# Keys of the first head group loaded in two transfers, its first queries cast and transposed in two pieces

## The chip, the cores and the metric

The kernel runs on one core of a Trainium2 chip. The metric is the device time of one execution in microseconds. The core's engines work side by side and meet at semaphores: PE (matmuls, with weight loads ahead of them), DVE and ACT (elementwise work, casts, transposes on DVE), POOL (elementwise work, and the issue of transfers that change the type on the way) and SP (which here only issues transfers). Each engine takes its instructions in the order in which the program holds them.

## The reference

Sigmoid attention over 8 batches of 12 heads with 448 positions and 64 columns, then a two-layer network on the 3584 tokens that come out:

```python
def _attn_ref(q, k, v):
    scores = scale * np.matmul(q, k.transpose(0, 1, 3, 2)) - np.log(S)
    attn = 1.0 / (1.0 + np.exp(-scores))
    return np.matmul(attn, v)

x = attn_out.transpose(0, 2, 1, 3).reshape(B * S, H * D)      # 3584 x 768

def _moe_ref(x, w_in, w_out, beta):
    h = x @ w_in                                              # 768 x 2048
    g = h * (1.0 / (1.0 + np.exp(-beta * h)))
    return g @ w_out                                          # 2048 x 768
```

All inputs and the output are float32; the kernel computes on float16 tiles with float32 sums.

## The kernel before

Heads are taken in groups of four, three groups to a batch, so that 128 partitions hold 4 heads times 32 rows. For a group, queries and keys lie in a `raw` tile of 128 partitions by 2 by 14 chunks of 64 columns: row r = 0 is the queries, r = 1 the keys, and `NB` = 14, `NH` = 7, `D` = 64. Before the scores can be formed, both are transposed by DVE in blocks of 32 (`transpose`, lines 200 and 212): the queries into `qT`, in halves of 7 chunks in the first group, the keys into `kT` by two instructions, the first over chunks 0 to 8, the second over chunks 8 to 14. `rows_of(0)` gives (0, 4), from which these 8 chunks come. A score matmul (L229) takes its weights from `kT` and streams `qT`; ACT turns score tiles in PSUM into float16 weights of the attention (`weigh`, L242, later `weigh_two`, L257); a further matmul with the values (L335) gives a tile of x, which DVE casts out of PSUM (L349). The two layers of the network (L379, L410, L524, L652) are woven between the score matmuls as filling work for PE, by a hand-written list of unit counts. Results leave through SP (L711).

The order of the start is written out by hand, inside a manual schedule, as the list `BEGIN`. Each entry is a few instructions on one or two engines, and entries stand in each engine's queue in this order:

- `("cast", r, c0, c1, act)` casts chunks c0 to c1 of group 0's keys or first half of queries from a float32 staging area (in the tile `gt`, which is not yet needed) into `raws[0]`, on ACT (L833) or DVE (L835).
- `("k", 0)` and `("q", 0, 0)` are the transposes of group 0's keys and of its first query half.
- `("idle", 20)` are 20 matmuls of 256 columns on zeros (L849), which need no input; they stand ahead of the first scores in PE's queue. `("busy", n)` are n such matmuls of 448 columns between scores (L854).
- `("scores", 0, h, s)` are score matmuls for query half h of group 0, with the ACT instructions behind them.
- `("beta",)` transposes the beta vector on DVE (L868).

Group 0's keys and first query half come in as float32 through SP's queue (L824); they are followed there by the beta vector (L856). All other loads (the second query half, the groups behind, the values, the weights) are issued by POOL (L125, L154, L169), with the keys of group 1 first.

Of the kernel before, what the change touches and what calls it, by code (L numbers as in the profile page):

```python
# [13 lines left out]
def kernel(  # L14
# [14 lines left out]
    B, H, S, D = q.shape  # L29
# [4 lines left out]
    HQ = P // BLK  # L34
    NB = S // BLK
# [106 lines left out]
    def rows_of(i: int):  # L142

        n = JF + int(i < KL // BLK)
        return i * JF + min(i, KL // BLK), n
# [14 lines left out]
    def double_v_last(b: int):  # L160
        assert all((b, "full", t, i) in ready for t in range(QPB) for i in range(KL // BLK))
        ready.add((b, "v"))
        nc.vector.tensor_copy(out=vs[b][KL:P, :, JF], in_=vs[b][0:KL, :, JF])
# [25 lines left out]
    def in_order(b: int, t):  # L189
        t = t.rearrange("p c e -> p (c e)").bitcast(FP32)  # L190
        return t.rearrange("p (q c) -> p c q", c=NB) if b == B - 1 else t

    def transpose(g: int, r: int, c0: int = 0, c1: int = NB):
        raw = raws[g][:, r]
        assert g or (r, c0) == (0, NB // 2) or all((r, "cast", c) in ready for c in range(c0, c1))
        if r == 0:
            if g not in qT:
                qT[g] = qTp.tile([P, NB * BLK, PAIR], FP16, tag="qT", name="qT")
            ready.update((g, "q", c) for c in range(c0, c1, NB // 2))
            nc.vector.transpose(  # L200
                out=in_order(g // QPB, qT[g][:, c0 * BLK : c1 * BLK]),
                in_=raw[:, c0:c1].rearrange("p c d -> p (c d)").bitcast(FP32),
            )
            return
        ready.add((g, "k"))
        kT[g] = kTp.tile([P, S, PAIR], FP16, tag="kT", name="kT")
        to = kT[g].rearrange("p k e -> p (k e)").bitcast(FP32)
        frm = raw.rearrange("p c d -> p (c d)").bitcast(FP32).rearrange("p (c f) -> p c f", c=NB)
        half = to.rearrange("p (x i q) -> p x i q", i=2, q=BLK)
        for i in (0, 2):  # L210
            c, n = rows_of(i)
            nc.vector.transpose(  # L212
                out=half[:, i // 2 :: 2].rearrange("p j i q -> p i j q"),
                in_=frm[:, c : c + 2 * n].rearrange("p (i j) f -> p i j f", j=n),
            )
# [78 lines left out]
    def half_visit(g: int, c0: int, second: int):  # L294
        slots = (2 * g, 2 * g + 1)
        scos = [score_tile() for _ in slots]
        plan = [(s, jt, sco, jt * QH) for jt in (0, 1) for s, sco in zip(slots, scos)]
        widths = [S, S]
        if second:
            plan = [(s, 2, sco, 0) for s, sco in zip(slots, scos)]  # L300
            plan += [(s, JF, scos[1], QH) for s in slots]
            widths = [QH, S]
        for i in range(0, len(plan), 2):
            for e in range(PAIR):
                for s, jt, sco, u0 in plan[i : i + 2]:
                    for hh in range(2):
                        score(sco, u0, s, jt, hh, e, c0, QH)
        if len(scored) == 2 and not second:
            two = weigh_two(ps[:, 0:4, 0:S], ())
            ats = dict(zip(map(id, scos), two if n_sc[0] % 2 == 0 else two[::-1]))  # L310
        else:
            ats = {id(sco): weigh(sco, n) for sco, n in zip(scos, widths)}
        for s, jt, sco, u0 in plan:
            at_use(ats[id(sco)], (s, jt, c0), slice(u0, u0 + QH))
# [3 lines left out]
    def attend(g: int, c0: int, n: int, keys=None):  # L318

        b, t = divmod(g, QPB)  # L320
        if b not in xTs:
            xTs[b] = xTp.tile([P, NHC, S], FP16, tag="xT", name="xT")
        assert (b, "v") in ready and (b, "full", t, HQ - 1) in ready
        slots = (2 * g, 2 * g + 1)
        if (g, c0) not in opened:
            opened[g, c0] = [bank(n, (g, s)) for s in slots], []
        avs, done = opened[g, c0]
        if keys is None:
            keys = [JF, *range(JF)] if n == S else [*range(JF), JF]
        for jt, i in [(jt, i) for jt in keys for i in range(2)]:  # L330
            s, av = slots[i], avs[i]
            at = at_take((s, jt, c0))
            base, nk = (last_base(s), KL) if jt == JF else (0, P)
            for hh in range(2):
                nc.tensor.matmul(  # L335
                    av[hh * D : (hh + 1) * D, 0:n],
                    vs[b][base : base + nk, 2 * (s % NPAIR) + hh, jt],
                    at[base : base + nk, hh, 0:n],
                    start=not done and jt == keys[0],
                    stop=len(done) + len(keys) > JF and jt == keys[-1],  # L340
                    tile_position=(base, hh * D),
                )
        done.extend(keys)
        if len(done) <= JF:
            return
        del opened[g, c0]
        for s, av in zip(slots, avs):
            touch(held.pop((g, s)))
            nc.vector.tensor_copy(out=xTs[b][:, s % NPAIR, c0 : c0 + n], in_=av)  # L349
        for s in slots:  # L350
            ready.update((b, s % NPAIR, c) for c in range(c0, c0 + n, QH))
# [433 lines left out]
    def fill_units(n: int):  # L785
        for _ in range(n):
            fill[at_fill[0]][1]()
            at_fill[0] += 1

    NH = NB // 2  # L790
    share_psum(3)
    with tc.manual_schedule():
# [27 lines left out]
        staged = gt[:, 0:4].rearrange("p c w -> p (c w)").bitcast(FP32)  # L820
        raws[0] = rawp.tile([P, 2, NB, D], FP16, tag="raw", name="raw")
        parts = {1: (staged, NB), 0: (staged[:, NB * D :], NH)}
        for r, (to, n) in parts.items():
            nc.sync.dma_start(  # L824
                out=to[:, 0 : n * D],
                in_=(q, k)[r][0, 0:HQ].rearrange("h (p c) d -> (h p) (c d)", c=NB)[:, 0 : n * D],
            )

        def cast(r: int, c0: int, c1: int, act: bool):
            out = raws[0][:, r, c0:c1].rearrange("p c d -> p (c d)")  # L830
            frm = parts[r][0][:, c0 * D : c1 * D]
            if act:
                nc.scalar.copy(out=out, in_=frm)  # L833
            else:
                nc.vector.tensor_copy(out=out, in_=frm)  # L835
            ready.update((r, "cast", c) for c in range(c0, c1))
# [10 lines left out]
        def idle_units(n: int):  # L847
            for _ in range(n):
                nc.tensor.matmul(idle[:, 0:256], still[:, 0:P], still[:, 0:256], start=True, stop=True)  # L849

        def busy_units(n: int):
            to = bank()
            for _ in range(n):
                nc.tensor.matmul(to, still[:, 0:P], still[:, 0:S], start=True, stop=True)  # L854
# [5 lines left out]
        def loads():  # L860
            for x in LATER:
                load(*x)

        def beta_columns():
            ready.add("beta")
            for i in range(P // BLK):
                part = slice(i * BLK, (i + 1) * BLK)
                nc.vector.transpose(out=beta_sb[part], in_=beta_in[:, part])  # L868

        BEGIN = [  # L870
            ("cast", 1, 0, 8, False), ("cast", 1, 8, 14, True), ("cast", 0, 0, 7, True), ("k", 0), ("q", 0, 0),
            ("idle", 20), ("scores", 0, 0, 1), ("busy", 2), ("scores", 0, 0, 0), ("busy", 2), ("busy", 4),
            ("q", 0, 1), ("q", 1, 1), ("scores", 0, 1, 0), ("busy", 4), ("busy", 4), ("q", 1, 0),
            ("scores", 0, 1, 1), ("busy", 2), ("beta",), ("k", 1), ("visit", 1, 0), ("busy", 1), ("v", 0),
# [7 lines left out]
        for what, *a in BEGIN:  # L882
            if what == "q":
                g, half = a
                transpose(g, 0, half * NH, (half + 1) * NH)
            elif what == "k":
                transpose(a[0], 1)
            elif what == "scores":
                half_visit(a[0], a[1] * QH, a[2])
            elif what == "cast":  # L890
                cast(*a)
            elif what == "idle":
                idle_units(a[0])
            elif what == "busy":
                busy_units(a[0])
            elif what == "v":
                double_v_last(a[0])
            elif what == "half":
                attend(a[0], a[1] * QH, QH)
            elif what == "values":  # L900
                attend(a[0], 0, S, a[1:])
            elif what == "visit":
                visit(*a)
            elif what == "dense":
                fill_units(a[0])
            elif what == "beta":
                beta_columns()
            elif what == "loads":
                loads()
            elif what == "two":  # L910
                share_psum(2)
# [152 lines left out]
```

## Time and profile before

| | |
|---|---|
| median of 3 runs | 369.52 us (369.27 to 369.52) |
| profiled execution, own time | 369.46 us |
| its span, first to last instruction | 367.7 us |
| PE busy | 362.2 us (99%) |
| DVE busy | 262.7 us (71%) |
| ACT busy | 258.5 us (70%) |
| POOL busy | 83.4 us (23%) |
| granted TensorE clock, mean | 0.999 |

The page gives busy time for each engine over the whole span, so a short stage has to be read from the trace itself: by windows (busy time of each engine in a stretch), by the chain of work that ended last, and by single instructions in order of time. In such rows the first number is the start and the second the length, in microseconds from the start of the span; a bracket tells how long the engine stood idle ahead of the instruction, and what ended that. SPq rows are issues of transfers, whose data lands later. Group rows give the busy time in microseconds and the mean of one instruction in nanoseconds.

### The profile page before, as it was taken

To read this page: it belongs to the slowest core of one execution; us is meant where nothing else is said; L and a number is where in the kernel's file an instruction comes from. 1 tells how busy PE (TensorE), PEld (TensorE's weight loads), DVE (VectorE), ACT (ScalarE), POOL (GpSimd) and SP (SyncE) were. 2 spreads that over 40 slices of the span, in tenths; PEclk is the share of its full clock that TensorE was granted. 3 is DMA by queue.
4 is the path that set the end of the run, shared out by engine and by line. 5 is a ranking of instruction groups with operands and counts; after the bars stand their busy time and mean duration, and the time that the engine had idled before them with its cause. 6 is when DMAs were issued, how large, how long until landed. Compare 5 with 4: busy or idle time off the path is not lost.

```text
span 367.7 us, 7007 instructions
## 1 busy us (share of the span) xinstructions
PE 362.2 (99%) x2756; PEld 175.9 (48%) x2756; DVE 262.7 (71%) x487; ACT 258.5 (70%) x306; POOL 83.4 (23%) x125
## 2 busy tenths in 40 slices
PE   8999999999999999999999999999999999999996
PEld 4434444434444455544444455554444455555664
DVE  3548765688988867785675976779766677687664
ACT  5987976999777588876877759887777758870000
POOL 7525343311310023331131003337000012210000
PEclk9999999999999999999999999999999999999999
DMA  8999999955292110096379221004903030002332
GB/s 166 204 207 202 205 205 202 225 65 89 40 167 57 44 45 1 1 170 140 52 128 167 55 50 37 1 2 68 214 34 86 2 87 0 1 2 65 89 102 89
DMA packets 32416, 34.62 MB, mean 94 GB/s; under 512 B 9328, under 2 KB 28416, under 8 KB 32384
## 3 DMA queue, kind: packets, MB, share of 16 engines
q0 software_dynamic: 26400, 22.47, 40.5%
q1 hardware_dynamic: 5984, 11.71, 11.6%
q8 instruction: 21, 0.34, 0.4%
q14 instruction: 11, 0.09, 0.1%
HBM read 45.62 MB, written 11.01 MB: 154 GB/s over the span
## 4 chain that ended last, share of the span: by engine, by line
PE 92%; DMA 3%; DVE 2%; ACT 1%; issue 0%; DVEq 0%; ACTq 0%
PE ps L652 34%; PE ps L524 26%; PE ps L229 12%; PE ps L335 10%; PE ps L379 6%; PE ps L410 3%; DMA raw<-in_q_dram 2%; PE ps L854 1%; ACT attns L257 1%; DMA gt<-in_k_dram 1%; DVE w_S L484 1%; DVE gt L397 0%; ACT attns L242 0%; DVE qT L200 0%; ACT sg L396 0%
## 5 line engine op out<-in xcount | busy, mean ns | idle before, releaser
L257 ACT ACTIVATE attns<-ps,nlogs 128x1792 f16<-128x1792 f32 x73 | 128.0, 1754 | 41.0 <-PE ps L229 40.8
L652 PEld LDWEIGHTS <-sum 128*128 128x128 f16 x536 | 48.9, 98 | 42.1 <-issue 13.7
L652 PE MATMUL ps<-w_T,sum 128*128 128x384 f16 (+2 forms) x328 | 58.1, 319 | 0.0
L538 POOL TENSOR_TENSOR gt<-attns,sg 128x448 f16<-128x448 f32 x21 | 23.9, 1137 | 146.0 <-ACT sg L535 146.0
L229 PE MATMUL ps<-qT,kT 32*128 32x448 f16 (+3 forms) x800 | 50.5, 353 | 1.1 <-ACT attns L242 0.5
L535 ACT ACTIVATE sg<-ps,beta_sb 128x448 f32<-128x448 f32 x72 | 45.1, 630 | 8.6 <-PE ps L524 5.9
L524 PE MATMUL ps<-xT,w_in 128*128 128x448 f16 x216 | 49.2, 353 | 0.0
L524 PE MATMUL ps<-xT,w_S 128*128 128x448 f16 x216 | 49.2, 352 | 0.0
L538 DVE TENSOR_TENSOR gt<-ps,sg 128x448 f16<-128x448 f32 x72 | 44.3, 619 | 2.3 <-ACT sg L535 2.2
L349 DVE CAST xT<-ps 128x448 f16<-128x448 f32 (+1 forms) x50 | 27.9, 599 | 25.2 <-PE ps L335 25.2
L671 DVE TENSOR_TENSOR osb<-ps,osb 128x384 f32<-128x384 f32 (+2 forms) x67 | 36.1, 540 | 12.1 <-PE ps L652 10.5
L524 PEld LDWEIGHTS <-w_in 128*128 128x128 f16 x288 | 28.0, 98 | 26.6 <-issue 0.7
L379 PE MATMUL ps<-xT,w_in 128*128 128x448 f16 x192 | 40.0, 353 | 0.0
L335 PE MATMUL ps<-attns,v 128*64 128x448 f16 (+3 forms) x400 | 39.9, 353 | 0.0
L638 DVE TENSOR_TENSOR sum<-gt 128x1024 f16<-128x1024 f16 x57 | 38.4, 690 | 0.2
L652 PE MATMUL ps<-w_out,sum 128*128 128x384 f16 x208 | 37.9, 327 | 0.0
L652 PE MATMUL ps<-w_out,gt 128*128 128x384 f16 (+2 forms) x200 | 36.6, 320 | 0.0
L585 DVE TENSOR_TENSOR ps<-ps,attns 128x448 f32<-128x448 f32 x24 | 15.2, 633 | 24.1 <-PE ps L524 24.1
L524 PEld LDWEIGHTS <-w_S 128*128 128x128 f16 x216 | 21.1, 98 | 19.4
L125 POOL DMA_DIRECT2D raw<-in_q_dram x24 | 13.3, 555 | 67.7 <-DVE kT L212 53.2
L379 PEld LDWEIGHTS <-w_in 128*128 128x128 f16 x192 | 17.5, 98 | 21.2 <-issue 6.8
L335 PEld LDWEIGHTS <-v 128*64 128x64 f16 (+1 forms) x400 | 17.8, 108 | 20.4 <-issue 13.0
(57 smaller groups left out, 345.8 us busy)
## 6 DMA issues: line engine op xcount, KB each, us to landing
out_dram<-osb SPq DMA_DIRECT2D x98, 96.0 KB, 1.9
raw<-in_k_dram POOLq DMA_DIRECT2D x23, 224.0 KB, 6.5
raw<-in_q_dram POOLq DMA_DIRECT2D x23, 224.0 KB, 6.0
v<-in_v_dram POOLq DMA_DIRECT2D x16, 192.0 KB, 7.7
w_out<-in_moe_w_out_dram POOLq DMA_DIRECT2D x4, 768.0 KB, 17.9
v<-in_v_dram POOLq DMA_DIRECT2D x16, 144.0 KB, 8.0
w_in<-in_moe_w_in_dram POOLq DMA_DIRECT2D x3, 512.0 KB, 11.0
w_in<-in_moe_w_in_dram POOLq DMA_DIRECT2D x3, 256.0 KB, 11.4
```

Of the source, the lines that this page charges most:

```text
L229: nc.tensor.matmul(sco[base : base + nk, hh, u0 : u0 + n], kT[g][lo : lo + BLK, jt * P : jt * P + nk, e], qT[g][lo : lo + BLK, c0 : c0 + n ...
L257: nc.scalar.activation(out=attns[:, slot : slot + 2].rearrange("p n h s -> p (n h) s"), in_=sco, func=AF.Sigmoid, bias=nlogs[:, 0:1], scal ...
L335: nc.tensor.matmul(av[hh * D : (hh + 1) * D, 0:n], vs[b][base : base + nk, 2 * (s % NPAIR) + hh, jt], at[base : base + nk, hh, 0:n], start ...
L349: nc.vector.tensor_copy(out=xTs[b][:, s % NPAIR, c0 : c0 + n], in_=av)
L379: nc.tensor.matmul(m1, w_in16[:, hc, dc * P : (dc + 1) * P], xTs[b][:, hc], start=fresh, stop=(hc == hi - 1), skip_group_check=lo > 0,)
L524: nc.tensor.matmul(out, w[:, c, i * P : (i + 1) * P], m[:, c], start=(start and c == 0), stop=(c == KH - 1), skip_group_check=not start,)
L535: nc.scalar.activation(out=sg, in_=h, func=AF.Sigmoid, bias=0.0, scale=beta_sb[:, dc : dc + 1])
L538: return lambda: engine.tensor_tensor(out=gt[:, dc, b % 2 * S : b % 2 * S + S], in0=h, in1=sg, op=ALU.mult)
L585: nc.vector.tensor_tensor(out=D, in0=B, in1=p5, op=ALU.add)
L638: nc.vector.tensor_tensor(out=sums[t, i], in0=x, in1=y, op=op)
L652: nc.tensor.matmul(m2, (x if op is None else sums[t, i])[:, dc], w[:, dc, lo:hi], start=first, stop=(dc == ND - 1), skip_group_check=i >= 4,)
L671: nc.vector.tensor_tensor(out=out, in0=in0, in1=in1, op=op)
```

## The change

The keys of group 0 are loaded by two transfers: chunks 0 to 8 (`K0` = 8), then chunks 8 to 14, both ahead of the first query half. The cast of that query half on ACT is done in two instructions (chunks 0 to 4 and 4 to 7), and so is its transpose on DVE, by a new entry `("part", g, c0, c1)` that calls `transpose` with those bounds. The key transposes stand between the casts and the query pieces as before.

```diff
         parts = {1: (staged, NB), 0: (staged[:, NB * D :], NH)}
-        for r, (to, n) in parts.items():
+        K0 = 2 * rows_of(0)[1]
+        for r, c0, c1 in ((1, 0, K0), (1, K0, NB), (0, 0, NH)):
             nc.sync.dma_start(
-                out=to[:, 0 : n * D],
-                in_=(q, k)[r][0, 0:HQ].rearrange("h (p c) d -> (h p) (c d)", c=NB)[:, 0 : n * D],
+                out=parts[r][0][:, c0 * D : c1 * D],
+                in_=(q, k)[r][0, 0:HQ].rearrange("h (p c) d -> (h p) (c d)", c=NB)[:, c0 * D : c1 * D],
             )
...
         BEGIN = [
-            ("cast", 1, 0, 8, False), ("cast", 1, 8, 14, True), ("cast", 0, 0, 7, True), ("k", 0), ("q", 0, 0),
+            ("cast", 1, 0, 8, False), ("cast", 1, 8, 14, True), ("cast", 0, 0, 4, True), ("cast", 0, 4, 7, True), ("k", 0),
+            ("part", 0, 0, 4), ("part", 0, 4, 7),
...
+            elif what == "part":
+                transpose(a[0], 0, a[1], a[2])
```

In the engines' queues this adds one transfer to SP, one cast to ACT and one transpose to DVE. DVE's cast of the keys waits for the first transfer alone, ACT's cast of the keys for the second, ACT's first query cast for the third. PE's instructions and their order stay the same.

## The prediction

> **What bounds the kernel now.** I read the page's totals first, then a table of engine busy time by stage, then the chain of waits at the start, then single instructions there.
>
> ```profile
> span 367.7 us, 7007 instructions
> ```
> ```profile
> 0.00:1.19 1.19, 0.00 (x0) 0.00 (x0) 0.33 (x2) 0.45 (x1) 0.34 (x6) 1.00 0.00 0
> 1.19:5.88 4.69, 4.27 (x21) 2.94 (x22) 1.61 (x5) 2.11 (x4) 4.58 (x8) 1.00 0.89 206
> 5.88:22.97 17.09, 16.60 (x200) 7.15 (x200) 7.85 (x23) 16.58 (x20) 8.43 (x14) 1.00 1.23 199
> 22.97:44.00 21.03, 20.94 (x140) 9.42 (x140) 15.05 (x29) 17.09 (x23) 8.48 (x13) 1.00 1.26 204
> 44.00:366.00 322.00, 320.43 (x2397) 156.36 (x2396) 237.84 (x431) 222.30 (x261) 61.59 (x86) 1.00 0.44 81
> ```
>
> Columns: window, length, busy time of PE, weight load, DVE, ACT and POOL with counts, granted clock, DMA share, GB/s. From 5.88 us on PE works almost without a break: 16.60 of 17.09, 20.94 of 21.03, then 320.43 of 322 (the last stretch holds the tail after the last matmul). From 5.88 to 22.97 ACT is full too (16.58 of 17.09). So the time is the moment at which real work starts, plus a nearly solid block; a start that moves by x moves the end by about x. The change touches only what lies ahead of 5.88, so that start is the whole question.
>
> ```profile
> 0.74 3.48 DMA gt<-in_k_dram
> 4.23 0.02 issue
> 4.25 0.44 DVE raw L835
> 4.69 0.02 issue
> 4.71 0.70 DVE kT L212 x2
> 5.42 0.42 DVE qT L200
> 5.83 0.04 issue
> 5.88 0.70 PE ps L229 x16
> ```
>
> This is the chain of waits (start, length, what). The keys' transfer lands at 4.22; DVE casts its share (8 of 14 chunks), turns the keys in two instructions and the queries in one, and PE starts. The chain names DVE alone, but ACT runs beside it and ends at the same moment:
>
> ```profile
> 4.25 0.51 ACT L833 CAST raw<-gt 128x384 f16<-128x384 f32 x1 [2.02 <-DMA gt<-in_k_dram]
> ```
> ```profile
> 4.81 0.56 ACT L833 CAST raw<-gt 128x448 f16<-128x448 f32 x1
> ```
>
> ACT's cast of the queries runs from 4.81 to 4.81 + 0.56 = 5.37; DVE's query transpose starts at 5.41, when DVE itself has just finished the keys (4.71 + 0.70 = 5.41). So two paths tie here, and shortening DVE's alone gains nothing.
>
> **The change part by part.** First the transfers.
>
> ```profile
> 0.74 0.38 SPq L824 DMA_DIRECT2D gt<-in_k_dram  x1
> 1.18 0.42 SPq L824 DMA_DIRECT2D gt<-in_q_dram  x1
> 1.65 0.42 SPq L856 DMA_DIRECT2D beta_in<-in_moe_beta_dram  x1
> ```
> ```profile
> gt<-in_k_dram SPq DMA_DIRECT2D x1, 448.0 KB, 3.5
> gt<-in_q_dram SPq DMA_DIRECT2D x1, 224.0 KB, 3.6
> beta_in<-in_moe_beta_dram SPq DMA_DIRECT2D x1, 8.0 KB, 4.2
> ```
> ```profile
> 2.75:3.75 1.00, 1.00 (x7) 0.69 (x6) 0.00 (x0) 0.00 (x0) 1.00 (x3) 1.00 0.97 332
> ```
>
> The issues go out 0.45 us apart, and the last column of the second view is the time to landing. The queries land at 1.18 + 3.6 = 4.78, only 0.56 after the keys: 229,376 bytes in 0.56 us is 410 GB/s. The 8 KB of beta takes longest of all. With the DMA engines 0.97 busy in the stretch 2.75 to 3.75, I read this as one queue that drains in order at the engines' pace. The keys in two pieces (256 KB, 192 KB) then land in this way: the second, and with it all keys, still near 4.22; the first earlier by its successor's 196,608 bytes at 410 GB/s, 0.48 us, so about 3.74. The queries, now third, are issued at 1.65 instead of 1.18 but wait for the same bytes as before. The added piece brings 128 more rows through the queue. The view has no price for a row; a floor is 0, a ceiling the whole step of 0.45 by which the issue is later. The queries' rows are half as long as the keys', yet moved at 410 GB/s, above the 332 of the stretch before; I stay near the floor and take +0.05 on the queries' landing. Beta moves back by 0.45 as well, to about 1.65 + 4.2 + 0.45 = 6.3; its first reader waits for nothing until
>
> ```profile
> 9.28 0.80 DVE L868 STREAM_TRANSPOSE beta_sb<-beta_in 32x32 f32<-32x32 f32 x4
> ```
>
> so it has 3 us of cover; without that it would hold DVE and the key transpose of group 1 behind it. SP has nothing else to issue before its first store. POOL's queue, with the other halves, isn't touched.
>
> Second, DVE's own path.
>
> ```profile
> L212 DVE STREAM_TRANSPOSE kT<-raw 128x256 f32<-128x256 f32 x1 | 0.4, 445 | 0.0
> L835 DVE CAST raw<-gt 128x512 f16<-128x512 f32 x1 | 0.4, 428 | 3.0 <-DMA gt<-in_k_dram 3.0
> L200 DVE STREAM_TRANSPOSE qT<-raw 128x224 f32<-128x224 f32 x1 | 0.4, 412 | 0.0
> L212 DVE STREAM_TRANSPOSE kT<-raw 128x192 f32<-128x192 f32 x1 | 0.3, 336 | 0.0
> ```
>
> The mean in ns follows the bar. The first transfer holds just the 8 chunks of DVE's cast and of the first key transpose, so these run at 3.76 to 4.19 and 4.22 to 4.67, half a microsecond ahead. The second key transpose reads the 6 chunks that ACT casts from the second transfer, and ACT ends those no sooner than before, 4.25 + 0.51 = 4.76; the transpose then takes 4.80 to 5.18. A lead of 0.48 has become 0.24, and DVE next waits for ACT's queries. Were the first piece not earlier at all, DVE's keys would end at 5.41 as now, and the two smaller query transposes would still end near 5.78; this edit is worth nothing alone, either way.
>
> Third, ACT and the queries. The two whole casts give 564 - 512 = 52 ns for 64 columns, 0.81 ns a column:
>
> ```profile
> L833 ACT CAST raw<-gt 128x448 f16<-128x448 f32 x1 | 0.6, 564 | 0.1
> ...
> L833 ACT CAST raw<-gt 128x384 f16<-128x384 f32 x1 | 0.5, 512 | 2.0 <-DMA gt<-in_k_dram 2.0
> ```
>
> so 256 columns cost 564 - 192 x 0.81 = 408 ns and 192 columns 356. Added up that is 764 where one cast had 564. How far neighbours overlap on ACT is seen in the stage behind:
>
> ```profile
> L242 ACT ACTIVATE attns<-ps,nlogs 128x896 f16<-128x896 f32 x18 | 16.5, 1016 | 0.1
> ```
>
> 18 x 1.016 = 18.29 us of instructions in 16.5 of busy time, 0.10 each. Those read PSUM, the casts SBUF; on DVE the two key transposes overlap by 0.445 + 0.336 - 0.70 = 0.08. I take 0.10: the pair needs 0.66 us, with 0.76 as the ceiling. [...]
>
> The transposes of 256 and 224 columns, 445 and 412 ns, give 1.03 ns a column: 313 for the first query piece, 280 for the second. From the start of ACT's query cast to PE, before: 0.56 + 0.04 (to DVE's start at 5.41) + 0.41 + 0.06 (to 5.88) = 1.07. After: the first piece is on DVE from 0.41 + 0.03 = 0.44 to 0.75, the second cast ends at 0.66, the second transpose can start as the first one drains, near 0.69, and ends near 0.97, and PE starts at 1.03. That gains 0.04; with no overlap anywhere it would be 0.76 + 0.03 + 0.28 + 0.06 = 1.13, a loss of 0.06.
>
> PE's instructions are the same ones; its first matmul waits for the whole half of the queries, so the split lets no score start sooner. The sum: +0.05 (landing) - 0.04 (pieces) = +0.01, with bounds from -0.04 (floor, with overlap) to +0.51 (0.45 + 0.06). The profiled execution took 369.46 us, 1.76 beyond its span, and stands 0.06 under the median of 369.52. So 369.47 against the profiled one, and 369.5 against the median.
>
> **The rivals.** (1) *The third issue sets the queries' landing.* If a transfer needs its 3.6 us from its own issue, the queries land 0.45 later, at 5.23, PE starts at 5.88 + 0.45 - 0.04 = 6.29, and the time is 369.46 + 0.41 = 369.9. For it: keys and queries have the same time to landing. Against it: half the bytes with the same time, and 8 KB with more, look like queueing.
>
> (2) *PE falls back to its slow pace* (the slower side). PE is kept busy ahead of the scores by 20 idle matmuls:
>
> ```profile
> 1.19 4.27 PE L849 MATMUL ps<-gt 128*128 128x256 f16 x20 [1.19 <-DVE gt L843]
> 5.88 0.70 PE L229 MATMUL ps<-qT,kT 32*128 32x224 f16 x16 [0.41 <-DVE qT L200]
> ```
> ```profile
> 9.34 1.62 PE ps L854 x8
> ...
> 23.02 0.57 PE ps L229 x6
> 23.59 1.43 PE ps L379 x7
> ```
>
> 20 of 256 columns in 4.27 us are 0.83 ns a column; 8 of 448 columns in 1.62 are 0.45, so the early pace is about half, though the granted clock reads 1.00 throughout. The 20 end at 5.46 whatever the loads do; a later start lengthens the pause of 0.41. If the longer pause sends PE back for as long as it took to leave that pace, 4.27 us, half of it is lost: 2.1 us, less up to 0.9 in which ACT still works on a tile (0.889 apart: 1.016 - 0.10), so 370.7 to 371.6. It decides from a pause above the longest that did no harm: 0.54, the wait below, with 7 matmuls at 0.20 each behind it. Rival 1's pause of 0.8 would pass it; mine of 0.42 doesn't. [...]
>
> (3) *ACT, not the landing, held the query cast.* ACT was free at 4.76 and began at 4.81; back to back it could have begun at 4.66. If the queries had in truth landed by then, the pair would start 0.15 sooner: 369.3. Against it: 1.18 + 3.6 = 4.78.
>
> (4) *The start and PE's second pause shrink together.*
>
> ```profile
> PE ps L229 <- ACT attns L242: 0.5, 1, 0.5
> PE ps L229 <- DVE qT L200: 0.4, 1, 0.4
> ```
>
> These are all of PE's waits from 5 to 30 us. Both gone is 0.95 at most: 368.5. For it, DVE is ahead on the keys; against it, nothing here feeds ACT faster, which sets the 0.5.
>
> **How the numbers follow.** My forecast (start within -0.05 to +0.25) has a chance of 0.46, rival 1 0.14, rival 3 0.10, rival 2 0.19, rival 4 0.11. About 0.2%, 0.74 us, is what a measurement of this kernel can tell from no change; forecast and rivals 1 and 3 lie inside it: 0.70. Slower is rival 2, 0.19; faster is rival 4, 0.11. The range holds 0.70 and the near parts of 4 and 2: 368.7 to 370.3. The forecast's own range is 369.4 to 369.8.
>
> **What would show it.** In the changed profile: DVE's cast near 3.75 instead of 4.25, followed by an idle stretch of DVE ahead of the second key transpose; ACT's first cast still at 4.25; ACT's first query piece at 4.8 to 4.9 (at 5.25 rival 1 is right, at 4.66 rival 3); the two casts 0.31 apart; PE's first score between 5.8 and 6.1; matmuls of 448 columns behind it 0.20 apart. A PE start more than 0.74 from 5.88, or a time that moves when the start doesn't, would make the reading wrong.

## The result, and the profile after

| | before | changed |
|---|---|---|
| median | 369.49 us (5 runs, 369.27 to 369.52) | 374.48 us (5 runs, 373.77 to 375.40) |
| profiled execution, own time | 369.46 us | 375.40 us |
| its span | 367.7 us | 373.6 us |

The ratio is 1.0139, with a 95% interval of 1.0122 to 1.0156: 5.0 us slower, far outside the forecast range. The chain of waits at the start of the changed kernel (start, length, what) shows where:

```profile
1.65 6.63 DMA gt<-in_q_dram
8.27 0.02 issue
8.30 0.41 ACT raw L834
8.71 0.02 issue
8.73 0.55 DVE qT L200 x2
9.28 0.04 issue
9.32 1.08 PE ps L229 x14
```

The queries, issued at 1.65, land at 8.28 and not near 4.8; PE's first score starts at 9.32 instead of 5.88, 3.44 us late. The transfers' view (size, time from issue to landing) sets them against the keys:

```profile
gt<-in_k_dram SPq DMA_DIRECT2D x1, 256.0 KB, 2.7
...
gt<-in_q_dram SPq DMA_DIRECT2D x1, 224.0 KB, 6.6
gt<-in_k_dram SPq DMA_DIRECT2D x1, 192.0 KB, 2.7
```

Both pieces of the keys are early, and DVE and ACT take them at once, as the instructions in order of time say (start, length):

```profile
3.45 0.50 DVE L836 CAST raw<-gt 128x512 f16<-128x512 f32 x1 [2.19 <-DMA gt<-in_k_dram]
3.98 0.82 DVE L212 STREAM_TRANSPOSE kT<-raw 128x256 f32<-128x256 f32 x2
```
```profile
3.88 0.51 ACT L834 CAST raw<-gt 128x384 f16<-128x384 f32 x1 [1.65 <-DMA gt<-in_k_dram]
8.30 0.66 ACT L834 CAST raw<-gt 128x256 f16<-128x256 f32 x2 [3.90 <-DMA gt<-in_q_dram]
```

The keys are ready at 4.80, 0.6 us before they were; then both engines stand for 3.9 us. Windows, in the columns used in the prediction, show what the transfers did meanwhile, first in the kernel before, then in the changed one; the third group is the changed kernel again and shows what PE did afterwards:

```profile
3.50:4.25 0.75, 0.75 (x6) 0.55 (x4) 0.00 (x0) 0.00 (x0) 0.75 (x2) 1.00 1.19 343
4.25:6.00 1.75, 1.34 (x13) 0.87 (x13) 1.54 (x4) 1.08 (x2) 1.75 (x4) 1.00 1.02 140
```
```profile
3.50:4.25 0.75, 0.75 (x6) 0.55 (x4) 0.72 (x2) 0.37 (x1) 0.75 (x2) 1.00 0.61 91
4.25:6.00 1.75, 1.20 (x7) 0.75 (x6) 0.55 (x2) 0.14 (x1) 1.75 (x4) 1.00 1.06 204
```
```profile
5.88:9.32 3.44, 0.00 (x1) 0.00 (x0) 0.59 (x3) 0.66 (x2) 1.23 (x3) 0.89 1.26 193
9.32:15.40 6.08, 6.08 (x57) 2.20 (x57) 2.69 (x10) 3.48 (x5) 3.81 (x6) 0.50 1.30 196
15.40:19.00 3.60, 3.60 (x39) 1.34 (x39) 0.00 (x0) 3.55 (x5) 1.75 (x3) 1.00 1.16 207
```

From 3.50 to 4.25 the kernel before moved 343 GB/s and the changed one 91, with the DMA share at 0.61. From 4.25 to 6.00 it is the other way, 140 against 204: the changed kernel's engines are busy then, but mostly with POOL's rows. (By the trace's records of single rows, 0.77 of the 16 engines' time from 3.30 to 6.57 went to POOL's rows and 0.24 to SP's.) And from 9.32 to 15.40 the granted clock is 0.50. The two losses add up at a place where both kernels do the same, the first matmuls with the values, before and changed:

```profile
12.88 0.92 PE ps L335 x16
```
```profile
18.91 0.92 PE ps L335 x16
```

That is 6.03 late: 3.44 from the start, which leaves 2.59 for the slow pace. The profiled executions differ by 375.40 - 369.46 = 5.94, so nothing else of size was lost or won behind.

### The profile page after: what moved, and what is told of

Its sections match the earlier page's. It is cut to its first block, busy times and chain, and to the rows that moved or that the text cites. A ratio compares the mean times of both kernels' runs of the same rounds, so it can differ in the third digit from the quotient of the medians.

```text
span 373.6 us, 7013 instructions
## 1 busy us (share of the span) xinstructions
PE 364.8 (98%) x2756; PEld 176.4 (47%) x2756; DVE 262.8 (70%) x488; ACT 259.2 (69%) x307; POOL 84.0 (22%) x125
## 4 chain that ended last, share of the span: by engine, by line
PE 95%; DMA 2%; ACT 2%; issue 1%; DVE 0%; SPq 0%; ACTq 0%
PE ps L652 33%; PE ps L524 26%; PE ps L229 12%; PE ps L335 10%; PE ps L379 9%; PE ps L410 3%; PE ps L855 2%; DMA gt<-in_q_dram 2%; ACT attns L257 1%; ACT attns L242 0%; ACT sg L396 0%; SPq L825 0%; DVE osb L671 0%; DVE qT L200 0%; ACT raw L834 0%
## 5 line engine op out<-in xcount | busy, mean ns | idle before, releaser
L652 PEld LDWEIGHTS <-sum 128*128 128x128 f16 x536 | 48.9, 98 | 42.1 <-issue 13.6
L229 PE MATMUL ps<-qT,kT 32*128 32x448 f16 (+3 forms) x800 | 51.6, 360 | 4.5 <-DVE qT L200 3.9
L671 DVE TENSOR_TENSOR osb<-ps,osb 128x384 f32<-128x384 f32 (+2 forms) x67 | 36.0, 539 | 11.9 <-PE ps L652 10.4
L229 PEld LDWEIGHTS <-kT 32*128 32x128 f16 (+1 forms) x800 | 13.0, 97 | 34.0 <-issue 32.5
```

The lines of the kernel that those rows point to most:

```text
L229: nc.tensor.matmul(sco[base : base + nk, hh, u0 : u0 + n], kT[g][lo : lo + BLK, jt * P : jt * P + nk, e], qT[g][lo : lo + BLK, c0 : c0 + n ...
L652: nc.tensor.matmul(m2, (x if op is None else sums[t, i])[:, dc], w[:, dc, lo:hi], start=first, stop=(dc == ND - 1), skip_group_check=i >= 4,)
L671: nc.vector.tensor_tensor(out=out, in0=in0, in1=in1, op=op)
```

## The experiments

Theory A was formed from this: the queries' rows come to the DMA engines later than POOL's first rows and have to share the engines with them, and PE then loses its pace. The rivals: B, a third transfer is slow in itself; C, the smaller pieces on ACT and DVE cost the time.

**Transfers alone, pieces alone.**

```diff
 # e1_transfers_only, against the changed kernel
-            ("cast", 1, 0, 8, False), ("cast", 1, 8, 14, True), ("cast", 0, 0, 4, True), ("cast", 0, 4, 7, True), ("k", 0),
-            ("part", 0, 0, 4), ("part", 0, 4, 7),
+            ("cast", 1, 0, 8, False), ("cast", 1, 8, 14, True), ("cast", 0, 0, 7, True), ("k", 0), ("q", 0, 0),
...
 # e2_pieces_only, against the changed kernel
-for r, c0, c1 in ((1, 0, K0), (1, K0, NB), (0, 0, NH)):
+for r, c0, c1 in ((1, 0, NB), (0, 0, NH)):
```

> The changed kernel with the query cast and transpose whole again; only the transfers are split. Theory A (the queries, as third transfer of SP's queue, reach the engines after a gap that POOL's transfers have entered, and share the engines with them from then on): the queries land 6 to 7 us after their issue as in the changed kernel, PE's first score at 8.5 to 10 us, time 373.5 to 375.5. Theory C (it is the pieces on ACT and DVE that cost): back to 369.3 to 369.8.

> The kernel before with the query cast and transpose in two pieces; the keys come in one transfer. Theory A: queries land near 4.8 us, PE's first score within 0.1 of 5.88, time 369.3 to 369.7. Theory C: 373 or more.

With the transfers alone: 374.45 us, ratio 1.0132 (1.0117 to 1.0147), queries landed 6.4 us after their issue. With the pieces alone: 369.58 against 369.53, ratio 0.9996 (0.9981 to 1.0011), PE's first score at 5.86. The whole loss is in the transfers; theory C is out, and the pieces are worth nothing measurable.

**POOL held back.**

```diff
 # e3_pool_later (2 copies) and f2_pool_later_still (4 copies), against the changed kernel
+spare = gt[:, NDC - 2, 0:512]
+for _ in range(2):
+    nc.gpsimd.tensor_copy(out=spare, in_=still)
...
 for x in LOADS:
     load(*x)
```

> The changed kernel, with two copies of 128x512 on POOL ahead of its first transfer, which hold that transfer back by about 1.2 us (a copy of this size took 0.62 us). Theory A: the queries, issued as late as in the changed kernel, find the engines free and land at 4.2 to 4.8 us; PE's first score at 5.4 to 6.0; time 369 to 371 (POOL's later loads may cost something behind). Theory B (a third transfer in one queue is slow in itself, or its late issue sets its landing, whatever POOL does): the queries land at 7 us or later, as in the changed kernel, time 373 or more.

> The changed kernel with four copies on POOL ahead of its first transfer in place of two, so that it goes out some 2.4 us later than in the changed kernel. Theory A: every engine is through the queries' rows before POOL's first ones come; the queries land at 4.2 to 4.6, against 5.47 with two copies, and PE's first score comes at 5.3 to 5.6. The time need not gain from it, since POOL's second query half (needed near 8.8) comes later too: 369 to 371.5. Theory B or B': queries at 5.4 or later.

POOL's first transfer went out at 2.43 and at 3.78 instead of 1.30. The queries, still third and still issued at 1.65, landed at

```profile
gt<-in_q_dram SPq DMA_DIRECT2D x1, 224.0 KB, 3.8
```

with two copies (5.47) and at 1.64 + 3.5 = 5.1 with four. In the kernel before they took 3.6, so nearly all that the changed kernel added to this (2.8 of 3.0 us) was POOL's doing, which B can't explain. Five of my numbers missed: with two copies the landing was 0.7 later than the 4.8 I allowed, PE's first score came at 6.51 and not by 6.0, and the time was 0.3 above 371; with four the landing was 0.5 later than the 4.6 I allowed, and the first score came at 6.13 and not by 5.6.

The times, 371.30 (ratio 1.0042, 1.0025 to 1.0059) and 371.29 (1.0048, 1.0031 to 1.0064), don't return to 369.5. The chain of waits with two copies, and behind it the same two places in the kernel before, show the larger part of the reason:

```profile
6.51 1.08 PE ps L229 x14
7.59 0.86 PE ps L855 x2
...
15.15 0.92 PE ps L335 x16
```
```profile
6.58 0.48 PE ps L854 x2
...
12.88 0.92 PE ps L335 x16
```

The first matmuls with the values are 2.27 late, and only 0.63 of this is the later first score. The other 1.64 is PE's slow pace (two matmuls in 0.86 instead of 0.48), behind a pause of only 0.87 us. With four copies these matmuls are 2.17 late (14.98 against 12.81 among the instructions in order of time), 0.25 of it from the first score, behind a pause of 0.49; there PE also waits 0.68 us more near 20 us, where POOL's loads arrive later. In both executions the 20 idle matmuls took 4.45 us instead of 4.27 and were at the slow pace to their end, and the trace's first clock record comes at 10.4 and 10.6: PE had not yet reached its full pace when the pause began. So these two times don't measure the landing alone.

**PE kept busy.**

```diff
 # e4_keep_pace, against the changed kernel
-            ("idle", 20), ...
+            ("idle", 56), ...
```

> The changed kernel with 56 idle matmuls ahead of the first scores in place of 20, so that PE has no long pause while it waits. If a part of the loss is PE's slow pace after its pause (rival 2): matmuls behind the first score run at 0.20 us each from the start, PE's first score stays near 9.3, and the time is 372.5 to 373.3, the late start of 3.4 us alone. If the pace costs nothing: 374 to 375.5 as in the changed kernel.

The chain of waits of this kernel, and a window behind its first score:

```profile
1.19 8.45 PE ps L850 x56
9.64 0.63 PE ps L229 x16
10.28 0.48 PE ps L855 x2
```
```profile
9.60:15.70 6.10, 6.10 (x83) 2.59 (x82) 2.45 (x9) 5.71 (x8) 4.08 (x6) 1.00 1.33 195
```

83 matmuls in 6.10 us, where the changed kernel did 57 in 6.08. The time is 373.14 us (1.0098, 1.0083 to 1.0113): of the 5.0 us, 374.48 - 373.14 = 1.3 go with the slow pace, and 373.14 - 369.49 = 3.65 are left with the late start (9.64 - 5.88 = 3.76). The 56 matmuls themselves hold the first score back here, to 9.64 where I expected it near 9.3. It is 0.32 later than in the changed kernel, so the slow pace costs nearer 1.34 + 0.32 = 1.66 us, an estimate that takes the medians from the runs and the 0.32 from the two traces.

**Which transfer, which queue.**

```diff
 # e6_queries_second: order of SP's issues
-((1, 0, K0), (1, K0, NB), (0, 0, NH))
+((1, 0, K0), (0, 0, NH), (1, K0, NB))
 # e5_queries_by_act: the queries by ACT's queue
-nc.sync.dma_start(
+(nc.sync, nc.scalar)[r == 0].dma_start(
 # f4_second_keys_by_act: the second keys by ACT's queue
-nc.sync.dma_start(
+(nc.sync, nc.scalar)[r == 1 and c0 > 0].dma_start(
 # e8_whole_keys_queries_by_act: as e5, with the keys in one transfer by SP
```

> The changed kernel with SP's order first keys, queries, second keys. Theory A (the third transfer of the queue finds POOL's rows ahead of it, whatever it carries): queries land near 4, the second keys at 6 to 8 us, ACT's key cast is then the late one, and the time is 373 to 375. If it is something about the queries' rows (their length or their place in memory): second keys by 4.5, time 369 to 370.

> The changed kernel with the queries' transfer issued by ACT ahead of its table load, at about 0.74 us, instead of third by SP. Theory A: no row of the queries has to wait for a third issue, so they share the engines with the keys alone and all three are in by 4.2 to 4.6 us; PE's first score at 5.4 to 5.9, time 369.0 to 369.6. Theory B (three transfers ahead of the scores are slow in themselves, from whichever queue): 373 or more.

> The keys in one transfer by SP, the queries by ACT at the same moment, the query cast and transpose in two pieces. Theory A: keys and queries share the engines from the start, both are in near 4.8 at the latest, since 672 KB at the 410 GB/s seen before need the same time in any order; the keys land later than 4.2, PE's first score at 5.7 to 6.2, time 369.2 to 369.9.

> The changed kernel with the second keys issued by ACT at 0.74, the first keys and the queries by SP as first and second. Theory A: nothing is issued later than 1.2, so all rows stand in the queues ahead of POOL's; first keys, second keys and queries land by 4.0 to 4.8, PE's first score at 5.6 to 6.1, time 369.1 to 369.9. Theory B: 373 or more.

With the queries second, it is the second keys that land 6.0 us after their issue, and the time is 375.06 us (1.0150, 1.0135 to 1.0166), just above the 375 that I allowed; which of the two the late transfer carries doesn't matter. With one transfer moved to ACT's queue, nothing is issued later than 1.2 and the loss is gone: 369.99 (1.0017, 1.0005 to 1.0028) with the queries there, 369.91 (1.0012, 1.0002 to 1.0022) with whole keys, 369.71 (1.0003, 0.9993 to 1.0012) with the second keys. So three transfers aren't slow in themselves. The first of these came out above the 369.6 that I expected: the second keys, now behind the queries, land at 4.73, and PE's first score is at 6.18, past the 5.9 I allowed. With whole keys the profiled execution took 371.50 and the ten others 369.87 to 369.97; in the profiled one the first score is at 6.36, past the 6.2 I allowed, and PE runs at its slow pace behind it (16 scores in 1.08 us). None beats the kernel before. The last one comes nearest to what the change asks for. In its profiled execution, the slowest of its ten with 370.39, the first score is at 5.62, 0.26 earlier, yet ACT's first tile starts at 6.22 against 6.29, since the 16 scores take 1.00 us there where they took 0.70. PE's waits from 5 to 30 us are

```profile
PE ps L229 <- DVE qT L200: 0.6, 1, 0.6
PE ps L229 <- ACT attns L242: 0.5, 1, 0.5
PE ps L335 <- DMA v<-in_v_dram: 0.2, 1, 0.2
```

The 0.4 ahead of the scores is gone, and 0.6 and 0.2 have come up where POOL's loads arrive later.

**Place or moment.** In these two the keys come in one transfer, as before, and the queries' issue is moved from 1.18 to 1.64 and 1.77: by putting beta's 8 KB ahead of it, or by a clearing on DVE for which SP waits. Two small clearings on DVE change places for it; POOL's first issue stays at 1.29.

```diff
 # e7_beta_between, against the kernel before (beta's clearing and transfer move ahead)
+nc.vector.memset(beta_in, 0.0)
 for r, (to, n) in parts.items():
...
+    if r:
+        nc.sync.dma_start(out=beta_in[0:NDC], in_=moe_beta.rearrange("(c p) -> c p", p=P))
 # f1_queries_second_but_late, against the kernel before (the other two clearings move ahead)
+still = gt[:, NDC - 1, 0:512]
+nc.vector.memset(still, 0.0)
+nc.vector.memset(beta_in, 0.0)
+nc.vector.memset(staged[:, NB * D : (NB + NH) * D], 0.0)
 for r, (to, n) in parts.items():
```

> The kernel before with the small beta transfer moved between keys and queries, so that the queries are third in SP's queue and issued 0.45 later, as in the changed kernel, but behind the whole 448 KB of the keys. Theory A (a gap between the rows of the short second piece and those of the queries lets POOL's rows in): the beta transfer has so few rows that the gap depends on the keys' rows still in the queue, up to 3.9 us; queries land at 4.6 to 5.3, time 369.3 to 370.5. Theory B (third place or the late issue alone sets it): queries at 6.5 or later, time 373 or more.

> The kernel before, keys in one transfer, queries second in SP's queue, with a DVE clearing of the queries' staging area ahead, for which SP waits: their issue moves from 1.18 to about 1.7 us, and nothing else changes place. Theory A in its mended form (what counts is whether the queries' rows stand in the engines' queues when POOL's first rows arrive, near 3.1 us; which place the transfer has does not matter): the queries land at 6 us or later, time 372.5 to 375.5. Theory B' (a third transfer in SP's queue is the trouble, wherever its moment is): queries at 4.8 to 5.3, time 369.4 to 370.2.

The first contradicted theory A as I had it: 375.18 us (1.0149, 1.0131 to 1.0168), although 448 KB of keys stood ahead of the queries. A gap behind a short piece isn't needed. The second then told place from moment; its chain of waits:

```profile
1.26 0.04 issue
1.31 0.44 DVE gt L826
1.75 0.02 issue
1.77 5.98 DMA gt<-in_q_dram
7.75 0.02 issue
7.77 0.57 ACT raw L837
```

Second in the queue, but 0.6 us late: 374.73 us (1.0135, 1.0118 to 1.0152). The moment of the issue decides, as against POOL's. The trace's records of single rows show the race (us; the queries have 128 rows; in the fourth line the second keys take their place):

```
                        issued   POOL's first row   rows started before it   landed   PE's first score
before                   1.18          3.82                79                 4.8          5.88
changed                  1.65          3.08                 0                 8.3          9.32
pieces only              1.17          3.87                99                 4.8          5.86
queries second           1.64          3.33                 0                 7.7          9.11
beta between             1.64          3.26                 0                 8.2          9.29
second but late          1.77          3.06                 0                 7.75         8.83
POOL later               1.65          4.06                88                 5.5          6.51
POOL later still         1.64          5.21               128                 5.1          6.13
```

## Why the prediction was wrong

The step that failed is the queries' landing: "The queries, now third, are issued at 1.65 instead of 1.18 but wait for the same bytes as before", with +0.05 on the landing and a ceiling of 0.45. I counted SP's bytes alone and dismissed the other queue in one sentence ("POOL's queue, with the other halves, isn't touched"). It isn't touched, but its rows run on the same 16 engines (0.77 and 0.24 of their time, above, add up to all of it), and its first transfer goes out at 1.30, in between the two moments of the queries' issue. In the kernel before, the queries' rows stood in the queues in time, and 79 of 128 were started before POOL's first; 0.47 later none was. The landing moved by 3.5 us, not 0.05. The row for it was in my reach: in the kernel before, POOL's first transfer, of the same 224 KB (though it changes the type on the way) and issued 0.11 later, took 5.7 us to land, and SP's 3.6.

In the changed kernel the queries' rows and POOL's are mixed from 3.3 us on (first rows at 3.30 and 3.08). In the kernel before, where POOL issued at the same moment (1.29 against 1.30), its first row came only at 3.82, when all 128 rows of the keys and 79 of the queries' had been started. So a run of rows that was queued before seems to pass first. That is read from a few traces, not tested by itself, and how the engines choose between the rows of two queues they don't show.

Rival 1 had the direction and the wrong mechanism: the landing isn't a fixed time from the issue (3.5 to 3.8 us and 6.6 with the same issue at 1.65, by what POOL does), so its 0.41 was about an eighth of the 3.44.

Rival 2, the slow pace, came true: a pause of 3.87 us, then 0.50 of the clock from 9.32 on. I priced it at 1.2 to 2.1 us; over the runs it is 1.3 to 1.7, in the profiled execution 2.59. Its point of decision, a pause above 0.54, did not hold: a pause of 0.49 had the slow pace behind it (POOL later still), and one of 0.55 the full pace (queries by ACT). In the changed kernel the recorded clock falls from 1.00 to 0.50 at 8.55, 3.1 us after the last idle matmul at 5.45. With POOL later, with POOL later still and with the transfers alone there is a slow pace without such a fall: the first clock records come only behind the pause, at 10.4, at 10.6 and after 13.6, so by the records PE had not reached its full pace before it. Why PE comes to its full pace sooner in some executions than in others (in the kernel before at 5.16) stays open. What I lacked was the 3.44 that caused the long pause. I treated a late landing and the slow pace as alternatives, and in the changed kernel they came together, one causing the other.

What held: the first keys land early (forecast 3.74, measured 3.43). The pieces on ACT stand 0.31 apart (8.30 and 8.61), as reckoned with the overlap, and from ACT's first query cast to PE it takes 9.32 - 8.30 = 1.02, forecast 1.03; the pair took 0.66, as forecast. "This edit is worth nothing alone" is borne out by the pieces alone. All keys landed at 3.86, not 4.22, and with the queries landing at 8.28 this gained nothing. Rivals 3 and 4 didn't occur. One reading was slightly off, and nothing hangs on it: with its own row of 336 ns the second key transpose would have ended at 5.14 and not at 5.18.

## What to carry to other kernels

The first transfers of this kernel race against those of another queue. Before a transfer is split or moved back by one issue (here 0.47 us), see when the other queues' first rows arrive, and keep what the first computation needs ahead of that moment, by a second issuing engine if need be (here that took the loss away, and gained nothing over the kernel before). A late start can also cost the pace of PE, here behind pauses from 0.49 to 3.87 us, so price both together. And when an edit's own parts come out near zero, ask what its order does to transfers that the diff doesn't name.

## What the runs showed of the hardware that was not expected

- A transfer of 224 KB lands 3.6 us after an issue at 1.18, and 6.0 us or more after one at 1.64 to 1.77, if POOL's first transfer is issued at 1.30. The late queries don't wait for slow rows of their own: from 3.30 to 6.57 117 of their rows were started, which took 0.10 us each, and beside them 246 of POOL's, about two for one, of which those of the same 1792 bytes took 0.21. Why the engines moved only 91 GB/s at first (3.50 to 4.25), why POOL's rows take twice as long, and why three of the 16 parts of the queries landed 0.6 to 1.7 us behind the others (13 by 6.57, the last at 8.27), stays open.
- The granted clock can read 1.00 while PE runs at half pace: in the kernel with the transfers alone, a window behind the first score reads

```profile
9.14:13.60 4.46, 4.46 (x39) 1.63 (x39) 2.69 (x10) 3.17 (x4) 2.81 (x5) 1.00 1.38 190
```

39 matmuls in 4.46 us, the same rate as the changed kernel's 57 in 6.08 at 0.50. The trace has no clock record there before 13.6 us, so the column shows the full clock for want of one. In the kernel before the first record is at 5.16, and the "1.00 throughout" that the prediction read beside the slow idle matmuls is of the same kind. The pace of the matmuls has to be read beside the clock.
- The recorded clock isn't the same from run to run: the changed kernel's five executions had mean clocks from 0.991 to 0.999, and times from 373.77 to 375.40. The mean doesn't rank them (0.995 at 373.77, 0.999 at 374.85), as it can't where records are missing.
